# Neighborhood attention on one NeuronCore: three loads of a band issued in pairs 1, 2, 3 instead of 0, 1, 2

## Chip, cores and metric

The kernel runs on one core of one Trainium2 chip. The metric is device time in microseconds of one execution; the median of the runs shown is used. Names: PE is TensorE (matmuls), ACT is ScalarE, DVE is VectorE, POOL is GpSimd, SP is the engine that issues most DMAs.

## The reference

A 224 x 224 image with 192 channels; each pixel attends to a 7 x 7 neighborhood with dilation 2, clamped at the borders. One head, output projection included.

```python
qkv = x @ wqkv
q, k, v = (qkv[..., :C].copy(), qkv[..., C:2 * C].copy(), qkv[..., 2 * C:].copy())
half = (ks - 1) // 2 * dil
off = jnp.arange(ks) * dil
r0 = jnp.clip(ir - half, 0, H - 1 - (ks - 1) * dil)
c0 = jnp.clip(ic - half, 0, W - 1 - (ks - 1) * dil)
...
kn = jnp.take_along_axis(kf, nidx, 1).reshape(B, H * W, ks * ks, C)
vn = jnp.take_along_axis(vf, nidx, 1).reshape(B, H * W, ks * ks, C)
scale = C ** (-0.5)
logits = jnp.einsum('bnc,bnkc->bnk', qf, kn) * scale
p = _softmax(logits, axis=-1)
o = jnp.einsum('bnk,bnkc->bnc', p, vn) @ wo
```

Since the dilation is 2, pixels of even and of odd rows never meet, nor those of even and odd columns: there are two row classes (`rc`) and two column classes (`cc`).

## The kernel before

**Tiling.** The image is cut into 14 bands of 16 rows (`NBAND`). The work runs in 14 band steps n (`steps`, L595): seven tiles of 16 rows of a class, each for both row classes. A step has seven pairs m = 0 to 6, a pair two strips s = 2m and 2m + 1 of eight columns. k counts the pairs over the whole run, so k = 7n + m.

**Data on the chip.** A band's pixels come in transposed, channels on partitions, by three DMA transposes (`load_items`, L146): 128 channels each into `XA[0]` (part 0) and `XA[1]` (part 2), rings of six bands, and the middle ones (part 1) into a tile `X1[b]` (two buffers), from which `xb_items` (L159) copies two halves into the rings `XB`. `sort_items` (L168) copies a band's rows of one class, part by part, into `XS[rc]` in the order that V needs. K isn't formed: Q is multiplied with the product of the weights (`AW`) to give `G` (tile names pg, pgh, gx, g), and the scores are `G` against the pixels `XA`, `XB`, on whose spare partitions marks add the borders of the neighborhoods. In the same way V is multiplied with the output weights (`WB`, `WP`) before attention, into `VF[rc]`.

**V and its shifts.** A strip's keys lie in two half tiles of rows. `VF[rc]` holds V for two groups of rows on partitions 0 to 63 and 64 to 127; `VD[rc]` holds the same shifted by a half. It is filled by DMAs from SBUF to SBUF: `vd_high` (L358, issued at L359) copies partitions 0 to 63 of `VF` to 64 to 127 of `VD`, in three parts: columns 0 to 7, 8 to 10 and 11 to 13. `vd_low` (L354, issued at L356) copies the other half of the old V before it is overwritten.

**One pair** (loop at L679): `stage1` computes the scores s and their negative maximum nmx for two strips, `stage1b` the exponentials p, `stage3` and `stage4` finish the pair two before (p times V into o_ps, division, output DMA), `stage2` transposes p of the pair before into pt_sb. Between them stand the preparations of the next step: parts of G (`gw`, `gh`) and two strips of V (`vs`) a pair, beginning three pairs into the step before (`LAG`). So the shift of columns 0 to 7 is issued in pair 6 of the step before (after `vs[7]`, L750), 8 to 10 in pair 1 of the step itself (after `vs[10]`), 11 to 13 in pair 2 (after `vs[13]`). Strip 7 is the first to read columns 8 to 10; its `stage3` runs in pair 5. Columns 0 to 7 are read from pair 2 on.

**What sets the order.** The program's order is kept on each engine (`in_order`), and each queue is served in order: an instruction that waits holds up all behind it on its engine. SP issues loads, shifts, most outputs. GpSimd does the copies of gx into G (L460, emitted in place, `halves`), and a list `pool_q` worked off at the end of each pair (`pool_do(max(4, len(add)))`): new copies and sorts (`add`) go to the front, and the small output DMAs of strip 0 (L593) wait behind them. Step 0 is prepared by hand: `PLAN` (L610) gives, pair by pair, the items of V (V for step 0, W for step 1) and of G (G for step 0, H for step 1), with the engine that evacuates each (d is DVE, a is ACT); N- is the second `stage4`, X a copy of `xb_items(2)`, T a `vd_high` on ACT's queue. `FIRST` (L619) names what GpSimd gets in the first 14 pairs: a to f are sorts (`SORTS`), x and y the copies of bands 3 and 4 into `XB`, k marks, g the constant rows of G for step 2 (`g_marks`).

**Loads.** In pair 0 of step n the list `ld` for band n + 3 is made (L703), and one load is issued in each of pairs 0, 1 and 2, ahead of that pair's items of V (L734).

Of the kernel before, what the change touches and what calls it, by code (L numbers as in the profile page):

```python
# [23 lines left out]
NBAND = 14  # L24
# [75 lines left out]
def kernel(  # L100
# [58 lines left out]
    def xb_items(b, eng):  # L159
        at = (16 * b) % (2 * RP) * S  # L160
        return [lambda m=m: eng(out=XB[m][XDAT[m]:XDAT[m] + 64, at:at + BND], in_=X1[b][XDAT[m]:XDAT[m] + 64, :]) for m in range(2)]
# [6 lines left out]
    def sort_items(b, rc, eng):  # L168

        hf = (b + rc) % 2  # L170
        return [lambda k=k: eng(out=_win(XS[rc], 0, 128, k * NSLOT * 128 + 64 * hf, [[128, NSLOT], [8, 8], [1, 8]]), in_=strip_in(b, rc, k))
                for k in (0, 2, 1)]
# [174 lines left out]
    def v_item(rc, cb):  # L347
        def emit(dve):
            pv = ps_g.tile([128, 512], F32, name="pv", tag="pg")
            v_mms(pv, lambda k, h: XS[rc][:, k, cb, 64 * h:64 * h + 64])  # L350
            evac(_win(VF[rc], 0, 128, AT[cb] * VP, [[193, 2], [1, C]]), pv[:, 0:2 * C].rearrange("p (t c) -> p t c", c=C), dve)
        return emit
# [5 lines left out]
    def vd_high(rc, c0, c1, eng=nc.sync):  # L358
        eng.dma_start(out=VD[rc][64:128, c0:c1, 0:VP - 1], in_=VF[rc][0:64, c0:c1, 0:VP - 1])  # L359
# [119 lines left out]
    def stage1(J, ab):  # L479
        s = 2 * J.m + ab  # L480
        s_ps = SS[ab]


        cols = {0: [(1, 7, S - 7), (8, 8, 0)], 2: [(1, 15, 9)]}.get(s, [(2, 14, 8 * s - 6)])
        lo = cols[0][0]
        for cc in range(2):
            units = []
            for h in range(2):
                u = []
                for (v, k0, n) in key_rows(J, h):  # L490
                    for (q, nq, c) in cols:
                        o = _win(s_ps, 64 * h, 64, cc * 256 + 16 * k0 + q, [[16, n], [1, nq]])
                        for pas in range(2):
                            X = (XA, XB)[pas][cc]
                            u.append((o, G[J.rc][cc][:, pas, s, 64 * h:64 * h + 64], _win(X, 0, 128, _x(J.rc, v, c), [[RW, n], [1, nq]]), pas))
                units.append(u)
            for q in range(max(len(u) for u in units)):
                for u in units:
                    if q < len(u):
                        (o, w, r, pas) = u[q]  # L500
                        nc.tensor.matmul(o, lhsT=w, rhs=r, start=(pas == 0), stop=(pas == 1))  # L501
        nmx = stat.tile([128, 2], F32, name="nmx", tag="nmx")
        nc.vector.tensor_reduce(out=nmx[:], in_=_win(s_ps, 0, 128, lo, [[256, 2], [16, 16 if J.n == 0 else 14], [1, 16 - lo]]), axis=AX.XY, op=ALU.max, negate=True)  # L503
        J.p = PP[J.rc][J.k % 2]
        J.s[ab] = (s_ps, nmx)
# [39 lines left out]
    def stage4a(J, ab):  # L545
        J.rs[ab] = stat.tile([128, 2], F32, name="rs", tag="rs")
        nc.vector.reciprocal(out=J.rs[ab][:], in_=J.o_ps[ab][:, C:C + 2])
        return J.rs[ab]
# [55 lines left out]
    def g_all(n):  # L604
        ti, rc = steps[n]
        its = [g_items(rc, ti, s0, ns) for (s0, ns) in GROUPS]
        return [it for (w0, w1, h) in its for it in (w0, w1)], [h for (w0, w1, h) in its]

    act, dve, pool = nc.scalar.copy, nc.vector.tensor_copy, nc.gpsimd.tensor_copy
    PLAN = (  # L610
        "Vd:0 Vd:1 Vd:2 Ga:2 Gd:3 Va:3 Gd:4 Va:4 Va:5",
        "Gd:5 Vd:6 Xd:0 Xa:1 Vd:7 Va:8 Va:9",
        "Va:10 N- Va:11 Ga:6",
        "Wa:0 Va:12 Wa:1 N-",
        "Hd:0 Wd:2 N- Ga:7 Va:13 Ha:1 Ha:2 Wa:3",
        "Ha:3 Wa:4 Wa:5 N-",
        "Wa:6 N- Wa:7 Ta:0:8 Hd:4",
    )
    FIRST = ("a", "bk", "", "", "cx", "d", "", "", "", "", "", "ge", "y", "f")  # L619

    def first_pool(c):
        if c in SORTS:
# [13 lines left out]
    LAG = 3  # L636
# [5 lines left out]
    def pool_do(n):  # L642
        for _ in range(min(n, len(pool_q))):
            pool_q.pop(0)()
# [10 lines left out]
    srt = sort_items(1, 0, dve)  # L655
# [21 lines left out]
    ld, gw, vs = [], [], []  # L677

    for k in range(NP + 2):  # L679
        J = pairs[k] if k < NP else None  # L680
        n = J.n if J else NSTEP
        w64, w128 = [], []
        if J:
            m = J.m
            nb, mb = divmod(k - LAG, 7)
            bg = k >= LAG and nb + 1 < NSTEP
            if bg and mb == 0:
                rcb = steps[nb + 1][1]
                gw, gh = g_all(nb + 1)
                vs = [v_item(rcb, cb) for cb in (0, 1, 2, 3, 4, 5, 6, 13, 7, 8, 9, 10, 11, 12)]  # L690
            if bg:
                w64 = gh[mb // 2:mb // 2 + 1] if mb % 2 == 0 else []
            if n == 0 and m < 3:
                w64 = gh0[m + 1:m + 2]
            if bg and n > 0:
                wg, wv = gw[mb + (mb > 1):mb + 1 + (mb > 0)], vs[2 * mb:2 * mb + 2]
                if nb == 0:
                    wg, wv = [it for it in wg if it not in gw[:AHEAD[1]]], [it for it in wv if it not in vs[:AHEAD[0]]]
                w128 = wg + wv
            stage1(J, 0)  # L700
            stage1(J, 1)
            stage1b(J, 0)
            if m == 0 and n + 3 < NBAND:  # L703
                ld = load_items(n + 3)
        if k == NP:
            stage2(pairs[k - 1])
        if k >= 2:
            stage3(pairs[k - 2], 0)
            stage3(pairs[k - 2], 1)
            if k >= NP:  # L710
                stage4a(pairs[k - 2], 0)
                stage4a(pairs[k - 2], 1)
            stage4(pairs[k - 2], 0)
            if k == NP - 1:
                stage4a(pairs[k - 2], 1)
        for it in w64:
            it(False)
        if J:
            stage1b(J, 1)
        if 1 <= k < NP:  # L720
            stage2(pairs[k - 1])

        if k >= 2 and n > 0:
            stage4(pairs[k - 2], 1)
        if not J:
            continue

        if m == 1 and 0 < n and n + 1 < NSTEP:
            vd_low(1 - J.rc, 7, 14)
        if n == 0 and m in (4, 6):  # L730
            vd_low(0, *((0, 4) if m == 4 else (4, 7)), nc.scalar)
        if 0 < n and m in (4, 5) and n + 2 < NSTEP:
            vd_low(J.rc, *((0, 4) if m == 4 else (4, 7)))
        if ld:  # L734
            ld.pop(0)()
        for w in PLAN[m].split() if n == 0 else ():
            (kind, by), at = w.split(":")[0], [int(c) for c in w.split(":")[1:]]
            if kind in "VWGH":
                {"V": v0, "W": vs, "G": gw0, "H": gw}[kind][at[0]](by == "d")
            elif kind == "N" and k >= 2:  # L740
                stage4(pairs[k - 2], 1)
            elif kind == "X":
                xb_items(2, act if by == "a" else dve)[at[0]]()
            elif kind == "R":
                vd_high(0, at[0], at[1], nc.scalar if by == "a" else nc.sync)
            elif kind == "T":
                vd_high(rcb, at[0], at[1], nc.scalar if by == "a" else nc.sync)
        for it in w128:
            it(False)
            if it is vs[7]:  # L750
                vd_high(rcb, 0, 8)
            if it is vs[10]:
                vd_high(rcb, 8, 11)
            if it is vs[13]:
                vd_high(rcb, 11, 14)
        if n == 1 and m == 2:
            p_zero(0)
        if n == 0 and m == 1:
            first_vd()
            g_row_on(1, 2, 12)  # L760
            g_col_on()
        if n == 0 and m >= 3:
            marks_on(m % 2, 2 * MM + 3 + (m - 3) // 2)
        add = [it for c in FIRST[k] for it in first_pool(c)] if k < len(FIRST) else []
        if n > 1:
            if m == LAG and n + 2 < NBAND:
                add = sort_items(n + 2, J.rc, pool)
            if m in (2, 4) and n + 3 < NBAND:
                srt = sort_items(n + 3, J.rc, pool)
                add = srt[:2] if m == 4 else xb_items(n + 3, pool) + srt[2:]  # L770
        pool_q[:0] = add
        if n == 12 and m == 1:
            last = ((0, 9, 0, 1), (9, 7, 9, 0))
            g_col(1, 6, 0, 1, pool)
            g_row(1, 6, 0, 1, pool, last)
            g_row(1, 6, 1, 13, pool, last[1:])
        pool_do(max(4, len(add)))
# [34 lines left out]
```

## Time and profile before

| | |
|---|---|
| median of 3 runs | 360.17 us (360.02 to 360.94) |
| profiled execution | 361.55 us |
| its span | 359.8 us |
| mean granted clock | 0.989 |
| TensorE busy 60 to 70 us, 70 to 80 us | 5.57, 9.78 us |
| granted clock there | 0.94, 0.72 |
| first s products of steps 1, 2, 3, 4, 5 | 46.98, 77.97, 100.35, 123.46, 147.13 us |
| of steps 6, 7, 8, 9, 10, 11 | 170.48, 193.02, 215.88, 239.25, 262.68, 286.04 us |
| one load on SP's queue, xa, x (median) | 2.58, 1.94 us |
| one shift on SP's queue (median) | 0.62 us |
| one output on SP's queue (median) | 0.56 us |
| GpSimd: one copy into XB, one sort (median) | 1.68, 0.93 us |
| GpSimd: one small output DMA (median) | 0.57 us |

How to read it: times of the trace are us from the span's start. In a timeline a row is start, duration, engine, line, operation, what is written from what, how many were merged; in brackets the engine's idle time before it and who ended it. An engine name with q is the engine's queue of DMAs and control. A row of the waits names who waited for whom, the total, how often, and the longest. The page's rows of digits cut the span into 40 slices of 9 us, each digit the busy share in tenths. In the chain of waits a time by "DMA" is a transfer under way that something waited for.

### The profile page before, as it was taken

The numbers are of one execution on the slowest core, as the hardware profiler recorded it, in microseconds if no ns is written. First come the engines' busy times: TensorE is split into PE (matmuls) and PEld (weight loads), VectorE is DVE, ScalarE is ACT, GpSimd is POOL, SyncE is SP. The second block draws the span as 40 slices with busy tenths as digits, with TensorE's granted clock in tenths as the row PEclk, the third lists the DMA queues.
The fourth block names the chain that finished last, engine by engine and source line by source line (L and its number), as shares of the span: only waits on it lengthen the run. The fifth ranks groups of instructions, "written<-read, shape, count | busy, mean of one in ns | idle before, by whom it ended". The sixth has DMA issues, their size and how long they took to land.

```text
span 359.8 us, 18502 instructions
## 1 busy us (share of the span) xinstructions
PE 332.8 (92%) x7628; PEld 302.1 (84%) x7628; DVE 308.1 (86%) x735; ACT 313.3 (87%) x832; POOL 280.1 (78%) x446
## 2 busy tenths in 40 slices
PE   4599989499999999999999999999999999999982
PEld 2478879389999879999998888889889999999872
DVE  8779889379999888998999889989898898998993
ACT  7669879379999889999999998989898899999993
POOL 8499999994977949949699497795987959483282
PEclk9999999879999999999999999999999999999999
DMA  8999977959989789798896988989979965652534
GB/s 179 214 141 198 152 157 145 191 132 186 191 162 194 157 197 193 158 205 188 153 203 163 191 182 180 180 188 183 195 159 202 176 150 126 136 124 73 121 83 92
DMA packets 136048, 59.35 MB, mean 165 GB/s; under 512 B 88882, under 2 KB 135439, under 8 KB 135964
## 3 DMA queue, kind: packets, MB, share of 16 engines
q1 hardware_dynamic: 129092, 55.33, 76.0%
q0 software_dynamic: 5280, 1.71, 2.8%
q10 hardware_dynamic: 1592, 1.15, 2.1%
q8 instruction: 59, 0.97, 1.2%
q14 instruction: 25, 0.20, 0.2%
HBM read 0.29 MB, written 19.27 MB: 54 GB/s over the span
## 4 chain that ended last, share of the span: by engine, by line
PE 59%; ACT 13%; DMA 13%; DVE 7%; SPq 4%; issue 2%; DVEq 0%; ACTq 0%
PE o_ps L541 12%; PE s L501 12%; DMA vd<-vf 11%; PE pg L425 9%; PE pt_ps L531 8%; PE pv L342 7%; ACT p L512 7%; PE pv L345 6%; PE pgh L425 5%; SPq L155 4%; DVE nmx L503 3%; ACT vf L335 2%; ACT gx L335 2%; ACT g L335 2%; DMA xa<-in_x_dram 1%
## 5 line engine op out<-in xcount | busy, mean ns | idle before, releaser
L512 ACT ACTIVATE p<-s,nmx 128x224 bf16<-128x224 f32 (+1 forms) x392 | 150.9, 452 | 19.7 <-DVE nmx L503 15.2
L503 DVE TENSOR_REDUCE nmx<-s 128x2 f32<-128x392 f32 (+3 forms) x196 | 103.4, 568 | 18.0 <-PE s L501 16.8
L460 POOL COPY g<-gx 64x512 bf16<-64x512 bf16 (+1 forms) x110 | 62.0, 564 | 56.8 <-ACT gx L335 52.8
L564 DVE TENSOR_TENSOR o_sb<-o_ps,rs 128x384 bf16<-128x384 f32 x169 | 94.2, 557 | 6.4 <-DMA out_dram<-o_sb 0.6
L335 ACT CAST vf<-pv 128x384 bf16<-128x384 f32 x197 | 88.9, 524 | 2.8 <-PE pv L345 2.5
L593 POOL DMA_DIRECT2D out_dram<-o_s x150 | 85.1, 573 | 1.0 <-issue 0.8
L541 PE MATMUL o_ps<-vd,pt_sb 128*64 128x193 bf16 x728 | 76.8, 247 | 9.4 <-DMA vd<-vf 6.9
L541 PE MATMUL o_ps<-vf,pt_sb 128*64 128x193 bf16 x840 | 83.2, 247 | 0.0
L501 PE MATMUL s<-xa,g 128*64 128x196 bf16 (+7 forms) x960 | 82.8, 236 | 0.3
L501 PE MATMUL s<-xb,g 128*64 128x196 bf16 (+7 forms) x960 | 82.3, 236 | 0.3 <-ACT g L335 0.3
L541 PEld LDWEIGHTS <-pt_sb 128*64 128x64 bf16 x1568 | 71.6, 109 | 12.2 <-issue 7.3
L501 PEld LDWEIGHTS <-g 128*64 128x64 bf16 x1920 | 78.4, 111 | 1.4 <-issue 0.9
L342 PE MATMUL pv<-wb,xs 128*64 128x384 bf16 x406 | 72.7, 333 | 5.6 <-ACT xs L370 3.5
L532 DVE COPY pt_sb<-pt_ps 128x1024 bf16<-128x1024 bf16 x94 | 64.5, 686 | 14.5 <-PE pt_ps L531 10.9
L345 PE MATMUL pv<-wp,xs 128*64 128x192 bf16 x812 | 73.1, 249 | 0.2 <-issue 0.2
L345 PEld LDWEIGHTS <-xs 128*64 128x64 bf16 x812 | 59.6, 111 | 9.5 <-issue 0.7
L531 PE MATMUL pt_ps<-ident,p 128*64 128x128 bf16 x1552 | 64.3, 220 | 0.0
L531 PEld LDWEIGHTS <-p 128*64 128x64 bf16 x1552 | 57.7, 110 | 5.4 <-issue 0.4
L335 ACT CAST g<-pg 128x512 bf16<-128x512 f32 (+3 forms) x138 | 58.8, 470 | 2.6 <-PE pg L425 2.6
L425 PEld LDWEIGHTS <-aw 128*64 128x64 bf16 x1320 | 55.2, 110 | 4.0 <-issue 1.6
L425 PE MATMUL pg<-xb,aw 128*64 128x512 bf16 (+9 forms) x440 | 55.2, 270 | 0.0
L425 PE MATMUL pg<-xa,aw 128*64 128x512 bf16 (+9 forms) x440 | 52.7, 271 | 1.4 <-DMA xa<-in_x_dram 1.4
(77 smaller groups left out, 351.9 us busy)
## 6 DMA issues: line engine op xcount, KB each, us to landing
out_dram<-o_sb SPq DMA_DIRECT2D x156, 96.0 KB
vd<-vf SPq DMA_DIRECT2D x37, 144.4 KB
vd<-vf SPq DMA_DIRECT2D x12, 385.0 KB
vd<-vf SPq DMA_DIRECT2D x12, 336.9 KB
vd<-vf SPq DMA_DIRECT2D x11, 192.5 KB
out_dram<-o_s POOLq DMA_DIRECT2D x78, 9.0 KB, 3.4
out_dram<-o_sb SPq DMA_DIRECT2D x13, 78.0 KB
out_dram<-xs SPq DMA_DIRECT2D x13, 78.0 KB
```

The lines of the kernel that those rows point to most:

```text
L335: nc.scalar.copy(out=out_, in_=in_)
L342: nc.tensor.matmul(pv[64 * h:64 * h + 64, 0:2 * C], lhsT=at(1, h), rhs=WB[:].rearrange("p t c -> p (t c)"), start=True, stop=False, skip_g ...
L345: nc.tensor.matmul(pv[64 * h:64 * h + 64, cc * C:(cc + 1) * C], lhsT=at(2 * cc, h), rhs=WP[(cc, 0)], start=False, stop=True, skip_group_ch ...
L425: nc.tensor.matmul(o, lhsT=l, rhs=r, start=(pas == 0), stop=(pas == 1))
L501: nc.tensor.matmul(o, lhsT=w, rhs=r, start=(pas == 0), stop=(pas == 1))
L503: nc.vector.tensor_reduce(out=nmx[:], in_=_win(s_ps, 0, 128, lo, [[256, 2], [16, 16 if J.n == 0 else 14], [1, 16 - lo]]), axis=AX.XY, op=A ...
L512: nc.scalar.activation(out=J.p[:, ab, cc, :, z:z + 8 * nr].rearrange("p q (r k) -> p q r k", k=8), in_=_win(s_ps, 0, 128, cc * 256, [[8, 2 ...
L531: nc.tensor.transpose(pt_ps[64 * h:64 * h + 64, 4 * ab + 2 * cc + q, :], J.p[:, ab, cc, q, 64 * h:64 * h + 64], ident[:])
L532: (nc.scalar.copy if J.n == NSTEP - 1 and 2 <= J.m < 5 else nc.vector.tensor_copy)(out=J.pt[:], in_=pt_ps[:])
L541: nc.tensor.matmul(o_ps[64 * h:64 * h + 64, cc * 193:cc * 193 + 193], lhsT=J.pt[:, 4 * ab + 2 * cc + q, 64 * h:64 * h + 64], rhs=V[h][:, A ...
L564: nc.vector.tensor_tensor(out=o_sb[:], in0=_win(o_ps, 0, 128, 0, [[194, 2], [1, C]]), in1=rs[:].unsqueeze(2).to_broadcast([128, 2, C]), op ...
L593: pool_q.append(lambda dst=dst, p=p, m=n * nj, cc=cc: nc.gpsimd.dma_start(out=dst.rearrange("j i c -> i j c"), in_=o_sb[p:p + m, cc, :]))
```

## The change

Four edits, all in the loop over pairs and its two tables.

```diff
-        "Vd:0 Vd:1 Vd:2 Ga:2 Gd:3 Va:3 Gd:4 Va:4 Va:5",
+        "Vd:0 Gd:2 Vd:1 Vd:2 Ga:3 Va:3 Ga:4 Va:4 Va:5",
         "Gd:5 Vd:6 Xd:0 Xa:1 Vd:7 Va:8 Va:9",
-        "Va:10 N- Va:11 Ga:6",
-        "Wa:0 Va:12 Wa:1 N-",
-        "Hd:0 Wd:2 N- Ga:7 Va:13 Ha:1 Ha:2 Wa:3",
-        "Ha:3 Wa:4 Wa:5 N-",
+        "Va:10 Va:11 N- Ga:6",
+        "Va:12 Wa:0 Wa:1 N-",
+        "Hd:0 Wd:2 Ga:7 N- Va:13 Ha:1 Ha:2 Wd:3",
+        "Wa:4 Wa:5 Ha:3 N-",
         "Wa:6 N- Wa:7 Ta:0:8 Hd:4",
     )
-    FIRST = ("a", "bk", "", "", "cx", "d", "", "", "", "", "", "ge", "y", "f")
+    FIRST = ("a", "bk", "", "", "x", "d", "c", "", "", "e", "", "g", "y", "f")
...
-        if ld:
-            ld.pop(0)()
         for w in PLAN[m].split() if n == 0 else ():
...
                 vd_high(rcb, 11, 14)
+        if ld and m > 0:
+            ld.pop(0)()
...
-            if m == LAG and n + 2 < NBAND:
+            if m == 3 and n + 2 < NBAND:
                 add = sort_items(n + 2, J.rc, pool)
-            if m in (2, 4) and n + 3 < NBAND:
+            if m in (4, 6) and n + 3 < NBAND:
                 srt = sort_items(n + 3, J.rc, pool)
-                add = srt[:2] if m == 4 else xb_items(n + 3, pool) + srt[2:]
+                add = srt[:2] if m == 6 else xb_items(n + 3, pool) + srt[2:]
```

- The loads of band n + 3 are issued in pairs 1, 2 and 3, and behind the pair's items of V and the shift that these release, instead of ahead of them.
- From step 2 on, the copies into `XB` and the sort of part 1 move from pair 2 to pair 4, the sorts of parts 0 and 2 from pair 4 to pair 6. The sorts of band n + 2 stay in pair 3.
- In `FIRST`, sort c moves from pair 4 to pair 6 and sort e from pair 11 to pair 9.
- In `PLAN`, G:2 is evacuated by DVE and comes second; G:3, G:4 by ACT; W:3 by DVE; V:12 and W:0, and W:4, W:5 and H:3 change places; three N- move by a place.

## The prediction, made before the change was run

> **What bounds the kernel now.** I read the page first, then the waits, then the timelines of TensorE, SP's queue and GpSimd around the longest wait.
>
> ```profile
> PE 332.8 (92%) x7628; PEld 302.1 (84%) x7628; DVE 308.1 (86%) x735; ACT 313.3 (87%) x832; POOL 280.1 (78%) x446
> PE   4599989499999999999999999999999999999982
> POOL 8499999994977949949699497795987959483282
> PEclk9999999879999999999999999999999999999999
> ...
> PE 59%; ACT 13%; DMA 13%; DVE 7%; SPq 4%; issue 2%; DVEq 0%; ACTq 0%
> ```
>
> TensorE sets the pace. Its row has one hole after the start, in the eighth slice (63 to 72 us), and the granted clock dips there and just after. In the chain DMA has 13%, nearly all shifts of V. GpSimd is full in the first nine slices and has room later. The waits name the hole:
>
> ```profile
> PE o_ps L541 <- DMA vd<-vf: 6.9, 6, 4.6
> ```
>
> 6.9 us in six waits, one of them 4.6. The TensorE timeline has that one in band step 1, pair 5:
>
> ```profile
> 65.34 0.25 PE L541 MATMUL o_ps<-vf,pt_sb 128*64 128x193 bf16 x1
> 70.22 0.32 PE L541 MATMUL o_ps<-vd,pt_sb 128*64 128x193 bf16 x1 [4.64 <-DMA vd<-vf]
> ...
> 70.66 0.68 PE L425 MATMUL pgh<-xa,aw 128*64 128x512 bf16 x2
> ...
> 75.74 0.25 PE L541 MATMUL o_ps<-vd,pt_sb 128*64 128x193 bf16 x1
> ```
>
> The shift that it waits for is columns 8 to 10 (L750). SP's queue and ScalarE's timeline show why it is late:
>
> ```profile
> 54.78 0.98 ACT L335 CAST vf<-pv 128x384 bf16<-128x384 f32 x2
> ```
> ```profile
> 56.42 1.84 SPq L155 DMA_TRANSPOSE x<-in_x_dram  x1
> 58.35 2.54 SPq L570 DMA_DIRECT2D out_dram<-o_sb  x3
> 60.99 0.68 SPq L356 DMA_DIRECT2D vd<-vf  x1
> 61.72 3.48 SPq L155 DMA_TRANSPOSE xa<-in_x_dram  x1
> 65.29 0.63 SPq L359 DMA_DIRECT2D vd<-vf  x1
> ```
>
> V was written at 55.76, but SP issued the shift at 65.29, behind the loads of pairs 0 and 1. It landed at 70.18 (chain: 4.89 us).
>
> **Part 1, the shift ahead of the loads, band step 1.** Without pair 0's load (1.84, with its gap 1.93) the three outputs and the low shift come 1.93 earlier, so the low shift ends at 59.74; the shift of 8 to 10 follows, at about 59.8 instead of 65.29, since pair 1's load is now behind it. Landings in the chain take 3.95 to 5.16 us: 63.8 to 65.0, before the need at 65.4 to 65.6. The 4.64 us go, and what follows them: from 70.22 to 75.74, 5.5 us, a 128x512 pair takes 0.68 where the same line takes 0.42 elsewhere. The work in it (six o_ps, pgh, transposes, pg, pv, s: 0.25+0.46+0.45+0.46+0.66+0.67 by the start-to-start times of the steps around) is 2.95 at full speed, so 2.6 to 2.8 more are lost. Together **7.4 us**, and step 2 could start at 70.6 instead of 77.97.
>
> **What takes its place: GpSimd.** While TensorE stood, GpSimd worked off its backlog:
>
> ```profile
> 66.43 0.87 POOL L255 COPY g<-ch 32x64 bf16<-32x64 bf16 x4
> ...
> 78.37 1.81 POOL L171 COPY xs<-xa 128x896 bf16<-128x896 bf16 x2
> 80.12 0.94 POOL L171 COPY xs<-x 128x896 bf16<-128x896 bf16 x1
> 81.00 1.29 POOL L460 COPY g<-gx 64x512 bf16<-64x512 bf16 x2
> 87.07 1.28 POOL L460 COPY g<-gx 64x512 bf16<-64x512 bf16 x2 [4.78 <-ACT gx L335]
> ```
>
> The copy that ends at 82.3 fills strips 6 to 9 of G for step 2, which TensorE reads in its pair 3, at 87.7 (the s products of the fourth pair after 77.97). The margin is 5.4 us, less than the 7.4 that TensorE would come earlier. From 41.5 to 82.3 GpSimd hardly idles (9.7, 9.8, 9.3 and 9.7 of 10 us). The diff reorders its work there but takes none of it away before this copy: FIRST holds the same sorts, copies and marks, and pool_do the same 15 and 10 output DMAs. So pair 3 of step 2 comes no sooner than about 82.3, less up to 1 us of idle time that could close, plus a wait of the copies into XB of band 3: their load goes from pair 2 (issued at 35.81) to pair 3, behind its outputs, at some 37.3 with one load less ahead. In a later step such a load, issued at 152.85, released its copy at 159.01, so it lands up to 6.2 us after issue: 43.5, where GpSimd is ready for it at 41.5 (sort c now comes later). I take 1 us of wait from 0 to 2. Gain: 87.7 - 82.3 - 1 = **4.4**, between 3.4 and 6.4 by these rows (7.4 if GpSimd doesn't hold, 0 if another wait takes it all). On the way the row marks of G (before: end at 69.7) come behind sort e, moved from pair 11 to 9 (2.74), with three output DMAs fewer ahead (0.57 each): 70.7, with the wait 71.7, against 70.6; about 1 us of the same delay falls there.
>
> **Part 2, later bands.** In steps 2 to 10 the same shift is issued 12.9 us into the step (113.24 in the step from 100.35) and needed at 17.4. In the new order SP issues it once V is written (107.3) and the pair's outputs and low shift are out, about 9 us in. Its stalls go: 0.55 at 118.3, 0.54 at 234.09, 0.62 at 257.51: **1.7 us**. Bounds: 0, and 2.3 if the two of 0.32 and 0.24 (200.55, 270.15) went too. These wait in pair 2 for columns 0 to 7, shifted in pair 6 before, which no load delays now; I count them unchanged.
>
> **Part 3, what is queued behind the moved loads.** Each load now stands ahead of the outputs of pairs 2, 3 and 4, the shift of 11 to 13 (needed a step later) and the low shifts of pairs 4 and 5 (overwritten a step later). By the rows (load 2.5, output 0.6, shift 0.65 us on SP) SP starts the first load some 9.6 us into a step, ends the third at 19.1 (before: 16 to 17) and reaches pair 6's shift at 24.1. Now that is at 24.9 to 26.0, mostly paced by the outputs' own data, so nothing is lost; with loads of 3.2 us it would be 26.2, up to 1.3 later. VectorE's output buffers (six, three pairs) have 10 us. Taken: 0, from +0.6 to -9 (1 us a step).
>
> **Part 4, GpSimd's copies and sorts two pairs later.** Copies at pair 4 find a load issued about 8 us earlier, sorts at pair 6 one of some 5 us. V reads the sorts from pair 3 of the next step, 4 pairs (13 us) on; GpSimd's idle time of 3 to 5 us a step (waits for gx: 4.93, 3.62) hides a late load. Without it each 1.8 us of two sorts would push the copies of G, which have as much slack. Taken: 0, within 1 either way.
>
> **Part 5, PLAN.** G:2 goes to VectorE (0.69), G:3 and G:4 to ScalarE (0.59 each), W:3 to VectorE (0.55 for 0.48). In the first pair both engines have idle gaps of 0.2 to 0.7 us at these lines. The moves of N- change no order within an engine but SP's. Taken: 0, within 0.7.
>
> **Sum.** The profiled execution took 361.55 (span 359.8 and 1.75 around it): 361.55 - 4.4 - 1.7 = 355.45, 6.1 less. The median shown, 360.17, is 1.38 below that execution; from it, **354.1 us**.
>
> **Rivals.**
> *GpSimd doesn't hold.* If pair 3 of step 2 can start without waiting, 7.4 + 1.7 = 9.1: 351.1. For: its spans are rough and some idle time closes. Against: the margin of 5.4 is read from two starts on the same clock.
> *A new wait with its own dip.* The trace has a wait of 1.02 us (ending at 51.27) with no dip behind it and one of 4.64 with a dip; the new one would be 1.7, or 2.7 if all falls at strips 6 to 9. If that dips too, up to 2.8 are lost: 4.4 - 2.8 + 1.7 = 3.3 less: 356.9. For: the wait for band 3's load, and sort e ahead of the marks. Against: the delay is split, and 1.7 lies nearer the row without a dip. The Trainium skill (TensorE: Matmul & The Clock Gate, "HAM oscillation") puts the point at idle gaps of about 3.4 us, which is against it too; the 4.64 us gap agrees, and no row here tests 2 to 4.
> *Slower: the shift of columns 0 to 7 becomes the late one.* It lands 4.6 to 5.1 us after issue and is needed 7.2 into the next step; issued 2.8 in (195.83) it already cost 0.32. Now the third load sits closer before it, on SP and in the DMA engines, which SP's queue (q1) fills to 76% on average. Every 0.1 later than 2.3 is lost in each of nine steps; from 0.68 a step (6.1 / 9) the gain is gone; at 1 us it is 9 - 6.1 = 2.9 over: 363.1. Against: by part 3 SP has drained by then.
> The Trainium skill (DMA: Bandwidth & Descriptors, "Queues, rings and completion order") has each DMA engine take descriptors in ring order, so bytes queued earlier delay a later transfer, which speaks for this rival; the landings of 4.6 to 5.1 beside 3.95 fit but do not prove it.
> *It doesn't do what it says*: if the shift of pair 1 waits for ScalarE or SP's outputs as long as now, nothing changes: 360. Against: V is written 9.5 us before the issue.
>
> **Chances.** Forecast 0.50 (own range 352.3 to 356.0), GpSimd free 0.12, new dip or a smaller gain 0.18, no change 0.07, slower 0.13. A run of this kernel tells about 0.3% (1.1 us) from no change. Faster 0.80, same 0.07, slower 0.13. The range takes the first three cases: 350.3 to 359.0.
>
> **What would show it.** The shift L359 of pair 1 ahead of the first load in each step, issued near 60 in step 1; no wait over 1 us for vd in pair 5, and no clock dip near 70; step 2 starting at 71 to 72; GpSimd's copy for strips 6 to 9 as TensorE's releaser near 83; steps of some 22.4 to 23.3 us later. Wrong: a wait over 3 us before 90, or waits for vd in pair 2 of most steps.

## The result and the profile after

| | before | after |
|---|---|---|
| median | 359.37 us (356.99 to 361.41, 20 runs) | 361.36 us (358.52 to 365.42, 20 runs) |
| profiled execution | 361.55 us | 358.52 us |
| its span, its mean granted clock | 359.8 us, 0.989 | 356.8 us, 0.997 |

The change makes the kernel slower: ratio 1.0069, 95% interval 1.0045 to 1.0094, 2.0 us in the medians. (Ratios, here and below, leave out executions more than 1.5% above the fastest of their kernel; medians and ranges take in all.) The two profiled executions say the opposite, and both are far from their medians: that of before is 2.2 us above, that of after is the shortest of its 20 runs. So a second profile of each kernel is used beside them (e1 and e5 below: spans 358.8 and 360.7, whose difference of 1.9 is close to that of the medians).

After, the page and the chain of waits:

```profile
PE 331.3 (93%) x7628; PEld 301.0 (84%) x7628; DVE 308.1 (86%) x735; ACT 312.6 (88%) x832; POOL 278.9 (78%) x446
...
PE   4699997988999989999999998999999999999982
...
POOL 8499699999969949779499694996968869483282
PEclk9999999999999999999999999999999999999998
...
PE 65%; POOL 10%; DMA 6%; ACT 6%; DVE 5%; SPq 3%; issue 2%; DVEq 0%; ACTq 0%; POOLq 0%
```

The hole in the eighth slice and the dip of the clock are gone. In the chain GpSimd has 10% where it had nothing: what ended last is now mostly GpSimd's work, from 48 to 85 us (in the second profile only up to 60 us). The waits of TensorE for V's shifts and for G:

```profile
PE o_ps L541 <- DMA vd<-vf: 4.7, 4, 1.6
...
PE s L501 <- POOL g L460: 1.8, 2, 1.5
```

4.7 us in four waits here, 7.0 in four in the second profile. SP's queue in step 1:

```profile
59.13 0.63 SPq L359 DMA_DIRECT2D vd<-vf  x1
59.85 2.73 SPq L155 DMA_TRANSPOSE x<-in_x_dram  x1
```

The shift of columns 8 to 10 is out at 59.13, ahead of the load, and nobody waits for it. GpSimd, in step 0 and in step 2:

```profile
44.69 3.39 POOL L161 COPY xb<-x 64x1792 bf16<-64x1792 bf16 x2 [3.16 <-DMA x<-in_x_dram]
...
83.53 2.62 POOL L460 COPY g<-gx 64x512 bf16<-64x512 bf16 x4
```

In brackets at 44.69: GpSimd stood 3.16 us until the load of band 3, now issued at 38.69, had landed. The four copies from 83.53 begin with the two for strips 6 to 9 of G, done at 84.81. And TensorE's waits, in the first profile of after and in the second:

```profile
58.70 0.28 PE L501 MATMUL s<-xb,g 128*64 128x196 bf16 x2 [1.53 <-POOL g L460]
...
73.46 0.28 PE L501 MATMUL s<-xb,g 128*64 128x196 bf16 x2 [0.40 <-POOL g L272]
...
81.68 0.24 PE L541 MATMUL o_ps<-vd,pt_sb 128*64 128x193 bf16 x1 [1.64 <-DMA vd<-vf]
...
128.56 0.24 PE L541 MATMUL o_ps<-vd,pt_sb 128*64 128x193 bf16 x1 [1.02 <-DMA vd<-vf]
...
221.45 0.24 PE L541 MATMUL o_ps<-vd,pt_sb 128*64 128x193 bf16 x1 [1.46 <-DMA vd<-vf]
```
```profile
83.99 0.24 PE L541 MATMUL o_ps<-vd,pt_sb 128*64 128x193 bf16 x1 [2.16 <-DMA vd<-vf]
...
130.92 0.24 PE L541 MATMUL o_ps<-vd,pt_sb 128*64 128x193 bf16 x1 [1.98 <-DMA vd<-vf]
...
224.42 0.24 PE L541 MATMUL o_ps<-vd,pt_sb 128*64 128x193 bf16 x1 [1.95 <-DMA vd<-vf]
```

The first two are waits for GpSimd. The others stand in pair 2 of a step and wait for the shift of **columns 0 to 7**, which before cost at most 0.83 us at a time there, and 1.01 in e1. All waits above 0.2 us in pair 2, with those that the profile puts down to nmx, come to 1.4 and 2.2 us in the two profiles of before and to 5.7 and 7.7 in those of after. What is ahead of the shift on SP's queue in step 3:

```profile
113.37 1.24 SPq L570 DMA_DIRECT2D out_dram<-o_sb  x2
114.66 3.04 SPq L155 DMA_TRANSPOSE xa<-in_x_dram  x1
117.80 1.19 SPq L570 DMA_DIRECT2D out_dram<-o_sb  x2
119.08 0.63 SPq L356 DMA_DIRECT2D vd<-vf  x1
119.80 1.69 SPq L570 DMA_DIRECT2D out_dram<-o_sb  x2
121.58 0.63 SPq L356 DMA_DIRECT2D vd<-vf  x1
122.30 1.20 SPq L570 DMA_DIRECT2D out_dram<-o_sb  x2
123.60 0.63 SPq L359 DMA_DIRECT2D vd<-vf  x1
```

Step 4 begins at 120.31. The rows from 114.66 on leave no gap: the third load, outputs, low shifts, and last the shift, 3.29 us into the step that needs it (before: 2.84). V was written at 121.35, so the shift left 2.25 us behind it. In steps 2 to 11 it left 0.3 to 2.1 us behind V in the two profiles of before, 0.7 to 6.1 in those of after.

Where the time went, by the first s products of steps 3 and 13:

| | step 3 begins | step 3 to step 13 | span |
|---|---|---|---|
| before, first profile | 100.35 | 231.5 | 359.8 |
| before, second (e1) | 98.54 | 232.3 | 358.8 |
| after, first profile | 97.26 | 231.4 | 356.8 |
| after, second (e5) | 99.32 | 233.3 | 360.7 |

Between the second profiles 0.8 us are lost up to step 3 and 1.0 after it.

### The profile page after: what moved, and what is told of

It is laid out like the page before. It is cut to its first block, busy times and chain, and to the rows that moved or that the text cites. A ratio compares the mean times of both kernels' runs of the same rounds, so it can differ in the third digit from the quotient of the medians.

```text
span 356.8 us, 18522 instructions
## 1 busy us (share of the span) xinstructions
PE 331.3 (93%) x7628; PEld 301.0 (84%) x7628; DVE 308.1 (86%) x735; ACT 312.6 (88%) x832; POOL 278.9 (78%) x446
## 4 chain that ended last, share of the span: by engine, by line
PE 65%; POOL 10%; DMA 6%; ACT 6%; DVE 5%; SPq 3%; issue 2%; DVEq 0%; ACTq 0%; POOLq 0%
PE o_ps L541 14%; PE s L501 13%; PE pg L425 10%; PE pt_ps L531 8%; PE pv L342 7%; PE pv L345 6%; PE pgh L425 5%; DMA vd<-vf 4%; POOL xs L171 3%; ACT p L512 3%; SPq L155 3%; POOL out_dram L593 2%; POOL g L460 2%; DVE nmx L503 2%; DMA xa<-in_x_dram 2%
## 5 line engine op out<-in xcount | busy, mean ns | idle before, releaser
L503 DVE TENSOR_REDUCE nmx<-s 128x2 f32<-128x392 f32 (+3 forms) x196 | 103.5, 568 | 19.1 <-PE s L501 17.6
L501 PE MATMUL s<-xb,g 128*64 128x196 bf16 (+7 forms) x960 | 82.3, 235 | 2.8 <-POOL g L460 1.8
L541 PE MATMUL o_ps<-vd,pt_sb 128*64 128x193 bf16 x728 | 75.5, 246 | 7.1 <-DMA vd<-vf 4.7
L541 PE MATMUL o_ps<-vf,pt_sb 128*64 128x193 bf16 x840 | 81.8, 246 | 0.0
L335 ACT CAST g<-pg 128x512 bf16<-128x512 f32 (+4 forms) x139 | 59.4, 470 | 2.1 <-PE pg L425 2.0
```

What stands on the lines that cost most here:

```text
L335: nc.scalar.copy(out=out_, in_=in_)
L541: nc.tensor.matmul(o_ps[64 * h:64 * h + 64, cc * 193:cc * 193 + 193], lhsT=J.pt[:, 4 * ab + 2 * cc + q, 64 * h:64 * h + 64], rhs=V[h][:, A ...
```

## The experiments

Medians of the runs, and the ratio to runs of the kernel before on the same chip.

| run | what it is | median, us | ratio (95%) |
|---|---|---|---|
| e1 | before, unchanged | 359.64 | 1.0013 (0.9984 to 1.0041) |
| e5 | the change, unchanged | 362.55 | 1.0112 (1.0047 to 1.0176) |
| e2 | loads behind the shift, still pairs 0, 1, 2 | 358.62 | 0.9996 (0.9970 to 1.0022) |
| e3 | the change from step 1 on | 360.80 | 1.0020 (0.9984 to 1.0055) |
| e4 | the change in step 0 only | 360.73 | 1.0053 (1.0020 to 1.0087) |
| e6 | the change, sort c ahead of x | 359.78 | 1.0037 (0.9989 to 1.0085) |
| e7 | the change, shift of 0 to 7 by ACT's queue | 358.23 | 0.9984 (0.9942 to 1.0026) |
| e8 | e2, sort f a pair later | 357.39 | 0.9964 (0.9921 to 1.0008) |
| e12 | before, sort f a pair later | 359.57 | 1.0027 (0.9993 to 1.0061) |
| e9 | the change with e6 and e7 | 358.33 | 0.9944 (0.9907 to 0.9982) |
| e10 | e9, sort f a pair later | 357.90 | 0.9955 (0.9921 to 0.9989) |
| e11 | e8, shift of 0 to 7 by ACT's queue | 354.09 | 0.9866 (0.9818 to 0.9914) |
| e13 | e10, loads in pairs 1, 2, 2 | 366.47 | 1.0187 (1.0149 to 1.0226) |
| e14 | e11, loads in pairs 0, 1, 3 | 352.56 | 0.9799 (0.9770 to 0.9829) |
| e15 | e10, loads in pairs 0, 1, 3 | 352.68 | 0.9863 (0.9809 to 0.9918) |
| e16 | the change, loads in pairs 0, 1, 3 | 360.91 | 1.0055 (1.0010 to 1.0101) |
| e17 | e14, loads in pairs 0, 2, 4 | 352.78 | 0.9861 (0.9798 to 0.9923) |
| e18 | e14, shift of 0 to 7 by SP again | 356.60 | 0.9962 (0.9919 to 1.0005) |

**Taking the change apart: e1 to e4.** e1 has no edit. e2 is the kernel before with the load moved behind the pair's items of V; e3 has the change's loop with the tables and loads of step 0 as before; e4 the reverse.

```diff
 e2
-        if ld:
-            ld.pop(0)()
...
                 vd_high(rcb, 11, 14)
+        if ld:
+            ld.pop(0)()
 e3 (the change's loop, the tables of before)
+        if ld and n == 0:
+            ld.pop(0)()
         for w in PLAN[m].split() if n == 0 else ():
...
+        if ld and n > 0 and m > 0:
+            ld.pop(0)()
 e4 (the loop of before, the change's tables)
-        if ld:
+        if ld and n > 0:
...
+        if ld and n == 0 and m > 0:
+            ld.pop(0)()
```

> The kernel before, unchanged, for a second profile. Theory D (the forecast took from one profiled execution a stall of 4.64 us and a clock dip of 2.6 to 2.8 us behind it, and the dip is not in most executions): the wait for the shift of columns 8 to 10 in step 1 is there again, 3 to 5 us, with the mean clock at 0.996 to 0.998 and no dip in most runs; time 358 to 360. Rival (the whole stall is rare): no wait over 1 us for vd near 66 us, time as now all the same.

> The kernel before with one edit: the load stands behind the pair's items of V and their shift, still in pairs 0, 1 and 2; tables, copies and sorts as before. If the shift ahead of the load is good by itself and only the later pairs cost: ratio 0.988 to 0.995 (the wait in step 1 falls from 4.6 to about 1 us, since pair 0's load is still ahead; the waits of pair 5, 1.7 us in all, go; those of pair 2 stay at about 1.4). If putting the shift first brings nothing: 0.998 to 1.002.

> The change from step 1 on only: loads in pairs 1, 2, 3 behind the shift, copies and sorts two pairs later; step 0's loads, PLAN and FIRST as before. Theory S (the loss is in the later steps: the third load keeps SP busy longer, and the shift of columns 0 to 7 reaches pair 2 late by 0.5 to 1.6 us a step): waits of pair 2 about 5 us in all, ratio 1.000 to 1.006, GpSimd no longer waits 3 us near 44. Theory F (the loss is in the first band, where GpSimd waits 3.2 us for band 3's load): ratio 0.985 to 0.993.

> The change in step 0 only: its loads in pairs 1, 2, 3 behind its items, and the new PLAN and FIRST; from step 1 on as before. Theory S: ratio 0.998 to 1.006 with waits of pair 2 as before (1.4 us in all). Theory F: 1.006 to 1.012, with GpSimd's wait of about 3 us near 44 us and its chain up to pair 3 of step 2, which then starts near 85 or later.

e1 shows how much of Part 1 was one execution's: its longest wait for vd is 3.32 us, not 4.64, and TensorE reads strips 6 to 9 at 85.90, not 87.70, so the margin over GpSimd's copy (done at 82.3 again) is 3.6 and not 5.4. e2 shows that the order behind the shift, without the later pairs, gains nothing that can be told (its wait in pair 5 of step 1 is still 2.14). The change's loss is split: e4, step 0's part alone, 0.5%; e3, the later steps alone, 0.2% and within its interval of nothing, though its profile (an execution of 362.53 us, 1.7 above its median) has seven waits for vd of 7.9 us in all.

**The change again, and its two suspects: e5, e6, e7.**

```diff
 e6
-    FIRST = ("a", "bk", "", "", "x", "d", "c", "", "", "e", "", "g", "y", "f")
+    FIRST = ("a", "bk", "", "", "c", "d", "x", "", "", "e", "", "g", "y", "f")
 e7
-                vd_high(rcb, 0, 8)
+                vd_high(rcb, 0, 8, nc.scalar)
```

> The changed kernel, unchanged, for a second profile and a comparison on the same chip as the next three. Theory S+F (the first band loses by GpSimd's wait for band 3's load, the later steps by a shift of columns 0 to 7 that lands late at pair 2): GpSimd waits 2 to 3.5 us near 44, waits of pair 2 for vd of 4 to 8 us in all, ratio 1.003 to 1.009.

> The changed kernel with sort c back in pair 4 and the copies x of band 3 in pair 6 (the two change places in FIRST), so that GpSimd has work while band 3's middle part lands. Theory F: the wait near 44 is gone, the copy for strips 6 to 9 ends 2.5 to 3.2 us earlier than in the changed kernel (82 to 82.5 for 84.9) and the time falls by 1.5 to 3 us: ratio 0.997 to 1.003. If the loss is all in the later steps: as e5 within 0.2%.

> The changed kernel with the shift of columns 0 to 7 issued from ScalarE's queue in all steps. Theory S by SP's queue: the shift no longer stands behind loads and outputs on SP, it is issued 1 to 3 us earlier, the waits of pair 2 for vd fall under 1.5 us in all, and the time falls by 2 to 5 us, less up to 0.6 us a step that ScalarE pays for issuing: ratio 0.994 to 1.003. If the transfer is late because the 16 DMA engines are behind: the waits stay at 4 us or more.

In e6 GpSimd hardly waits for the load of band 3 any more (0.4 us), but TensorE waits 6.8 us for vd all the same, and the ratio can't be told from that of the change. In e7 the waits for vd fall from 7.0 us to 0.3, and the ratio from 1.0112 to 0.9984: the shift of columns 0 to 7 is the larger loss. A new wait appears, TensorE for gx (4.2 us in five). The chain of waits of e7 around step 3 shows its cause:

```profile
117.54 3.65 DMA out_dram<-o_sb
```
```profile
118.93 0.90 ACT L335 CAST vf<-pv 128x384 bf16<-128x384 f32 x2
121.26 0.60 ACTq L359 DMA_DIRECT2D vd<-vf  x1
121.91 0.79 ACT L512 ACTIVATE p<-s,nmx 128x224 bf16<-128x224 f32 x2 [2.08 <-DVE o_sb L564]
```

V is written at 119.83; ScalarE's issue of the shift waits until 121.2, when an output that SP issued at 117.54 has landed, and ScalarE stands idle for 2.08 us before the p behind it (the bracket names VectorE, which had long been done). In e7's trace the DMAs that SP and ScalarE issue take eight semaphores in turn, and before each stands a wait on its own one, that is for the landing of the eighth DMA before it in the program's order; for this shift that is the output right behind the third load. Six of the 13 shifts stood so behind V, up to 2.41 us and 7.2 in all.

**GpSimd's backlog: e8 and e12.**

```diff
 e8 (on e2) and e12 (on before)
-    FIRST = ("a", "bk", "", "", "cx", "d", "", "", "", "", "", "ge", "y", "f")
+    FIRST = ("a", "bk", "", "", "cx", "d", "", "", "", "", "", "ge", "y", "", "f")
```

> e2 (loads behind the shift, still in pairs 0 to 2) with sort f moved from pair 13 to pair 14, behind the copy of G for strips 6 to 9 of step 2. Theory G (GpSimd's chain holds step 2, so that the stall removed in e2 gave nothing): that copy ends at 79 to 80 for 81.9, pair 3 of step 2 starts 1.5 to 2.7 us earlier than in e2, and the time falls by 1 to 2.5 us against e2: ratio 0.992 to 0.997. If GpSimd does not hold: as e2, 0.998 to 1.001.

> The kernel before with sort f in pair 14 and nothing else. Theory G: as long as TensorE stands for the shift in step 1, GpSimd catches up there and its order does not matter: ratio 0.997 to 1.002, the copy for strips 6 to 9 ends near 79.5 and TensorE does not come for it before 85. If sort f alone is worth what e8 gained: 0.993 to 0.997.

Sort f stands ahead of the copy for strips 6 to 9. GpSimd in e2 and in e8:

```profile
80.65 1.28 POOL L460 COPY g<-gx 64x512 bf16<-64x512 bf16 x2
```
```profile
77.76 1.28 POOL L460 COPY g<-gx 64x512 bf16<-64x512 bf16 x2
```

The copy starts 2.9 us earlier. But TensorE waited for it in neither run: pair 3 of step 2 began at 84.29 in e2, 2.4 us after the copy was done, and at 82.69 in e8, 3.7 us after; and step 2 had begun 1.8 us earlier in e8 before the copy ran. So theory G isn't borne out. On the kernel before, the later sort f buys nothing (e12); with the load behind the shift the ratio is 0.9964, just within its interval of nothing (e8). That sort f's place is worth anything is not shown.

**Mended versions: e9, e10, e11.** e9 joins e6 and e7, e10 adds sort f in pair 14; e11 is e8 with the edit of e7, that is the kernel before with three edits: load behind the shift, f a pair later, shift of columns 0 to 7 by ScalarE.

```diff
 e9 (on the change) and e11 (on e8)
-                vd_high(rcb, 0, 8)
+                vd_high(rcb, 0, 8, nc.scalar)
 e9 (on the change)
-    FIRST = ("a", "bk", "", "", "x", "d", "c", "", "", "e", "", "g", "y", "f")
+    FIRST = ("a", "bk", "", "", "c", "d", "x", "", "", "e", "", "g", "y", "f")
 e10 (on e9)
-    FIRST = ("a", "bk", "", "", "c", "d", "x", "", "", "e", "", "g", "y", "f")
+    FIRST = ("a", "bk", "", "", "c", "d", "x", "", "", "e", "", "g", "y", "", "f")
```

> The changed kernel with both mendings: sort c in pair 4 and the copies x in pair 6 (e6), and the shift of columns 0 to 7 from ScalarE's queue (e7). If the two losses are separate they add: 2.8 + 4.3 below e5 (362.55), some 355 to 357, ratio 0.987 to 0.993. If the second only moves the wait: as e7, 0.996 to 1.000.

> e9 with sort f moved from pair 13 to 14 as in e8. Theory G (GpSimd's chain up to the copy for strips 6 to 9 holds step 2): up to 2.7 us earlier there, 354 to 356, ratio 0.984 to 0.991. If step 2 is held by something else by then: as e9.

> e8 (loads behind the shift in pairs 0 to 2, sort f later) with the shift of columns 0 to 7 from ScalarE's queue: does the move to pairs 1 to 3 bring anything at all? If it does not, e11 is as e10 or better, 0.985 to 0.992, waits for vd under 2 us in all; if the later pairs help, e10 is ahead by 1 us or more.

All three intervals lie below 1 (by the medians of all runs e9 and e10 are only 0.6 and 1.0 us faster than before). The expectations of e9 and e10 were missed: the two losses don't add up, and the later sort f brings nothing. But e11, whose loads, copies and sorts are two pairs (sorts, copies) or one pair (loads) earlier than in e10, and whose step 0 has the tables of before, is 3.8 us ahead of it. So something in the later pairs or the tables still cost.

**Which part of the later pairs: e13 to e18.** The loads are moved, in e14 together with the sorts that read the third one.

```diff
 e13 (on e10)
         if ld and m > 0:
             ld.pop(0)()
+        if ld and m == 2:
+            ld.pop(0)()
 e14 (on e11; sorts of parts 0 and 2 go to pair 6 with the third load)
-        if ld:
+        if ld and m != 2:
...
-            if m in (2, 4) and n + 3 < NBAND:
+            if m in (2, 6) and n + 3 < NBAND:
...
-                add = srt[:2] if m == 4 else xb_items(n + 3, pool) + srt[2:]
+                add = srt[:2] if m == 6 else xb_items(n + 3, pool) + srt[2:]
 e15 (on e10) and e16 (on the change)
-        if ld and m > 0:
+        if ld and m != 2:
 e17 (on e14)
-        if ld and m != 2:
+        if ld and m % 2 == 0:
 e18 (on e14)
-                vd_high(rcb, 0, 8, nc.scalar)
+                vd_high(rcb, 0, 8)
```

> The version mended in three places (c ahead of x, the shift of columns 0 to 7 from ScalarE's queue, sort f in pair 14), whose loads go out in pairs 1, 2, 3 (357.9 us, ratio 0.9955), with the third load moved to pair 2, right behind the second; tables, copies and sorts stay. In the compiled program the DMAs of the hardware queues take eight semaphores in turn, and each waits until the eighth DMA before it in the program has landed; for the shift on ScalarE's queue that is the first output of pair 4, which followed the third load directly. Theory 1 (that output's landing holds ScalarE): with two outputs between them it lands earlier, ScalarE's idle time before the p behind this shift falls from about 2 us to under 1 in most steps, TensorE's waits for gx (4.8 us in all) to under 2.5, and the ratio comes near 0.987 (0.983 to 0.991). Theory 2 (copies and sorts two pairs later, or loads behind pair 0, cost as such): the ratio stays near 0.9955 (0.993 to 0.999), whatever ScalarE's wait does.

> The best version (loads in pairs 0, 1, 2 behind the shift, shift of columns 0 to 7 from ScalarE's queue, sort f in pair 14; 354.09 us, ratio 0.9866) with the third load alone moved to pair 3, and with it, from step 2 on, the sorts of parts 0 and 2 that read it, from pair 4 to pair 6; copies into XB stay in pair 2. Theory 1 (the output right behind the third load lands late and holds ScalarE's shift): ScalarE idles 1.5 to 2.5 us before the p behind this shift in several steps, TensorE waits for gx after it, and the ratio goes back toward 0.9955 (0.991 to 0.999). Theory 2 (the first two loads and the copies set it): it stays at 0.983 to 0.990.

Both of these theories fell: e13, meant to free ScalarE's issue, lost 8.6 us against e10, and e14, meant to bring the wait back, was the fastest so far. ScalarE's issue did come sooner in e13: in step 3 0.46 us after V was written (e10 1.70), and over the 13 shifts it stood 6.4 us behind V (e10 11.0). Yet the time rose. The waits of e13 and of e14 name what took its place:

```profile
DVE o_sb L564 <- DMA out_dram<-o_sb: 17.8, 11, 3.9
...
PE o_ps L541 <- DVE pt_sb L532: 9.7, 8, 2.9
```
```profile
DVE o_sb L564 <- DMA out_dram<-o_sb: 0.6, 2, 0.5
```

VectorE waited 17.8 us, up to 3.9 at a time, for a free output buffer: the outputs stood behind two loads in a row, 5.11 us of SP's queue in step 3. Then pt_sb, which VectorE copies later in the same order, came late, and TensorE waited for it. In e10 VectorE's wait was 8.7 us (6.8 in e9, which differs by sort f alone), in e11 5.6, in e14 0.6. That gave a third theory, the distance between the loads. The Trainium skill (DMA: Bandwidth & Descriptors, "Queues, rings and completion order") has each DMA engine consume descriptors in ring order, by which bytes queued earlier would delay a later transfer. e13 agrees with it: from 95 to 275 us an output right behind a load landed 4.5 us after its issue, the fourth one behind 2.9 (medians). Distance isn't all, though: the kernel before has its loads in pairs 0, 1, 2 too, ahead of the items, and VectorE waited 0.6 and 0.8 us there.

> The change mended in three places (copies into XB in pair 4, sorts in pair 6, the change's tables; 357.9 us, ratio 0.9955 with loads in pairs 1, 2, 3) with loads in pairs 0, 1, 3. Against the version of 352.56 us it differs in the copies' place and in step 0's tables. Theory 3 (how close the loads stand on SP's queue sets how long VectorE waits for a free output buffer: 17.8 us in all with loads in 1, 2, 2, 8.7 in 1, 2, 3, 5.6 in 0, 1, 2, 0.6 in 0, 1, 3): VectorE waits under 1.5 us for out_dram, ratio 0.978 to 0.986. Theory 2 (copies and sorts two pairs later cost as such, or the tables): ratio 0.989 to 0.996 though VectorE's waits are gone.

> The change itself, nothing mended, with its loads in pairs 0, 1, 3 instead of 1, 2, 3. Theory 3 (closeness of the loads): the outputs and the shift of columns 0 to 7 come forward, VectorE's waits for output buffers fall under 1.5 us, the waits for vd in pair 2 from 7 (second profile of the change) to under 3, ratio 0.985 to 0.993. Rival (the shift of columns 0 to 7 stays late on SP's queue, whatever the loads' distance): vd waits stay at 4 to 7, ratio 1.000 to 1.008.

> The version of 352.56 us (loads in pairs 0, 1, 3) with loads in pairs 0, 2, 4, as far apart as a step has them. Theory 3: VectorE's waits for output buffers stay under 1 us; little is left to gain, ratio 0.977 to 0.984. Rival (the last load's place ahead of pair 6's shift): the outputs of pairs 5 and 6 and ScalarE's shift come behind it, ScalarE waits for the landing of the eighth DMA before, ratio 0.986 to 0.995. In step 0 sort d reads the third load one pair after its issue, so GpSimd may idle some 3 us there.

> The version of 352.56 us with the shift of columns 0 to 7 back on SP's queue. Theory 3: with the loads apart SP reaches that shift in time, vd waits under 2.5 us, ratio 0.980 to 0.986. Rival (the queue of the shift is what counts): vd waits of 4 to 7 us in all, ratio 0.990 to 0.999.

e15 has the change's later copies and sorts and its tables, and is as fast as e14 (352.68 and 352.56 us; VectorE waits 1.8). So the later copies and the tables cost nothing that can be told, and the loads' pairs alone are worth 3 to 5 us against e10 (medians 357.90 and 352.68 on two chips, ratios 0.9955 and 0.9863). (Over all runs of the kernel before beside them, medians 359.28 and 359.62, e14, e15 and e17 all come to 0.981.) e18 shows that the shift's queue counts too: back on SP, 4.0 us are lost (medians on two chips), as its rival had it. e16 shows that spread loads alone don't rescue the change: 1.0055, with four waits of 4.0 us for vd, and two for GpSimd of 2.0; its expectation of 0.985 to 0.993 was wrong, and the rival's 1.000 to 1.008 came true. e17 spreads the loads further and gains nothing more. In step 0 GpSimd stands 3.28 us for band 3's last load, issued at 43.06, before its copies into `XB`; step 3 begins at 98.94 (in e14 at 96.28), and its later steps are the shortest (226.5 us from step 3 to 13; e14 227.1).

## Why the prediction was wrong

**Right: the mechanism of Part 1.** The shift left at 59.13 (59.8 said), the 4.64 us went, step 2 began at 71.76 (71 to 72 said), and in the first profile GpSimd was the next bound: its marks, written from 71.95 to 73.41, brought two short waits, and the chain of waits runs through its work until the copy for strips 6 to 9.

**Wrong: Part 1's size, "Gain: 87.7 - 82.3 - 1 = 4.4".** Each of its numbers came out worse. 87.7 was one execution's: 85.90 in the second profile. The copy was done at 84.81 and 85.56 instead of 83.3, since the wait for band 3's load, taken as 1 of 0 to 2, was 3.16 and 3.70: the load was issued at 38.69, not 37.3, and took 6 us. Pair 3 of step 2 began at 84.36 and 86.67. So the gain at that point was 3.3 between the first profiles, and a loss of 0.8 between the second. In the second it wasn't the copy that held TensorE, since pair 3 began 1.1 us after it was done. VectorE stood for an output buffer in pair 0 of step 2:

```profile
73.79 0.56 DVE L564 TENSOR_TENSOR o_sb<-o_ps,rs 128x384 bf16<-128x384 f32 x1 [2.50 <-DMA out_dram<-o_sb]
```

The output that it waited for, issued at 69.30 right behind the second load, took 4.39 us to land; and in pair 2 came the 2.16 us for the shift of columns 0 to 7. Both belong to Part 3. e4, with the change in step 0 alone, where pair 5 of step 1 still waits (3.09 us), costs 0.5%, so nothing in step 0's own part pays for it.

**Right: Part 2.** In pair 5 of the steps behind step 1 no wait for vd is left. The 1.7 us don't show in the time all the same, because longer waits in pair 2 came in their place: from step 3 to 13 the first profiles take 231.5 and 231.4 us, the second 232.3 and 233.3.

**Wrong: Part 3, "Taken: 0, from +0.6 to -9".** This is the step that turned the sign. Its own reckoning had SP reach pair 6's shift at 24.1 us of a step, or 26.2 with loads of 3.2 us. In the step from 97.26 the loads took 2.67, 2.40 and 3.04, the first began at 9.2, the third ended at 20.4 (19.1 said), and the shift came at 26.3. The third load was followed without a gap by eight other DMAs ahead of the shift, so nothing was drained by then, which is what the argument against the third rival had rested on. The waits in pair 2 came to 5.7 us in the first profile, in six steps (two of them the profile puts down to nmx), and to 7.7 in the second, up to 2.16 at a time; not in nine steps, but longer where they came. e7 takes these waits away alone, and the ratio goes from 1.0112 to 0.9984. So the third rival, given 0.13, was what happened: its mechanism and place, with 2.0 us over the median before where it had said 2.9 over its own base.

**Wrong, and hidden until the shift was mended: Part 3's "VectorE's output buffers (six, three pairs) have 10 us".** Outputs behind loads that follow each other closely land so late that these buffers run out: VectorE waited for one 3.1 us in the second profile of the change (not at all in the first), 8.7 in e10, 17.8 in e13.

**Not contradicted: Parts 4 and 5**, at nothing. e15 against e14 tests the later copies and the tables (but for c, x and f), with the loads out of each other's way. The sorts of parts 0 and 2 are in pair 6 in both; no run moves them alone.

**The base.** The sum was made against an execution 2.2 us above the median of 20 runs, whose long stall was itself part of what the sum took away. The 1.38 taken off at the end repaired the base, not the gain.

The best versions, e14, e15 and e17, are 7 us faster than before by their medians. They keep from the change that a load stands behind the shift (e15 all but its loads' pairs, the place of c, x and f, and the shift's queue), and none has its loads in three neighbouring pairs. No run combines the shift of columns 0 to 7 on ScalarE's queue with loads ahead of the pair's items, as they were before; so what the change's own idea is worth in these versions is not shown.

Why loads in pairs 0, 1, 2 (e11) disturb less than in 1, 2, 3 (e10), though they are as close, is in part in the traces. In e11 ScalarE issued each of the 13 shifts 0.03 us after V was written, since the eighth DMA before had landed; in e10 eight of them stood, up to 3.28 us and 11.0 in all. That and VectorE's wait for output buffers come to 24.2 us in e13, 19.7 in e10 and 5 to 6 in e11, e14, e15 and e17 (one execution each), which is the order of their times, but for the 1.3 to 1.5 us that e11 is behind the last three. How much of the time each of the two costs stays open.

## What to carry to other kernels

Before a DMA is moved on a shared queue, lay out the whole period of that queue behind it, at the long durations and not at the medians: what counts is when the last transfer on it that has a deadline gets out, and how long the buffers that drain through it can be held. Spread bulk loads over the period with the small urgent transfers between them, and give the one with the tightest deadline another queue (here worth 1.3% on the change, and 1.1 to 1.6% on the best version). Spreading paid here only with that: on the change itself it brought nothing that can be told (e16). And price a stall from more than one execution: a wait seen at 4.64 us in one profile was 3.32 in the next.

## What the runs showed of the hardware

**The clock.** The prediction weighed the rule of the Trainium skill (TensorE: Matmul & The Clock Gate, "HAM oscillation") that puts the dip at idle gaps of about 3.4 us. The runs don't bear out a sharp point: dips came after 3.32 us (e1) and 3.09 (e4), and in e3 after a gap of 2.00 us ending at 81.07, while gaps of 2.14 (e2), 2.32 (e10) and 2.44 us (e11) left the clock at 1.00. Two stretches of e3 (from and to, length, the busy times of PE, PEld, DVE, ACT and POOL; the last three numbers are granted clock, DMA share and GB/s):

```profile
70.00:80.00 10.00, 7.67 (x162) 6.11 (x157) 8.51 (x20) 7.51 (x20) 9.80 (x11) 1.00 0.83 174
80.00:90.00 10.00, 8.93 (x173) 7.95 (x175) 5.98 (x15) 6.31 (x19) 7.68 (x14) 0.83 0.99 191
```

TensorE was busy 7.67 us of the ten before, but how busy it was before doesn't sort these cases either: in e13 a gap of 2.03 us ending at 170.95, with 7.97 us busy in the ten before, was followed by a granted clock of 0.66 over 5 us, and in e11 the gap of 2.44 us, with 6.78 busy, by 1.00. What sets the dip stays open.

**The spread.** Executions of one kernel differ by 4 us (the 20 runs of before; 8 in the round of e1) to 7 us (the change), more than the 2.0 us between the medians; the two profiles of each show different stalls of different lengths. Loads further apart don't make the spread small by themselves: e14 has 351.35 to 353.08 (five runs) and e15 352.52 to 353.46 (six), but e17 351.67 to 357.58 (six).
